# Banded attention and a rational MLP on one core: an issue order planned with slack between the engines

## The chip, the cores and the metric

The kernel runs on one core of a Trainium2 chip. A core has five engines that run their own instruction streams in order: TensorE (PE; its weight loads are shown apart as PEld), VectorE (DVE), ScalarE (ACT), GpSimd (POOL) and SyncE (SP), which here only issues DMAs. They wait for each other on semaphores. The metric is the device time of one execution in microseconds (us), the median of several.

## The reference

Attention over 8 batches, 8 heads, 576 positions and 64 dimensions in float32, causal with a window of 128 and a linear bias by head, and on its result, 4608 tokens of 512 numbers, an MLP with 2048 hidden numbers and a rational function in place of an activation:

```python
scores = scale * np.matmul(q, k.transpose(0, 1, 3, 2))
mask = (rel >= 0) & (rel < window)
scores = np.where(mask, scores + bias[None], -1000000000.0)
attn = softmax(scores)
x = (attn @ v).transpose(0, 2, 1, 3).reshape(B * S, H * D)
h = x @ w_in
P = a[0] + a[1] * h + a[2] * h2 + a[3] * h3
Q = 1.0 + np.abs(b[0]) * np.abs(h) + np.abs(b[1]) * h2
out = (P / (Q + 1e-06)) @ w_out
```

## The kernel before

The tokens are 36 blocks of 128. The MLP takes them in 17 tiles (3 blocks, 15 times 2 blocks, 3 blocks); the attention in units of one pair of heads and one or two blocks, for the most part four units for each MLP tile. While the MLP of tile t runs, the attention of tile t + 1 runs in between and writes x (x_hi and x_lo) for it.

To keep float32 accuracy at a faster matmul, numbers are split into a high part and a remainder, and a product takes three matmuls (high by high, high by low, low by high). The weights come as 64-bit words in memory. For tile 0 they are converted to float32 chunk by chunk (`convert`, L554 to L557, 32 steps k: even ones w_in, odd ones w_out) and used as such. Then `split` (L571, L572) makes the high part on ScalarE and the remainder on VectorE or GpSimd, 32 steps again, while tile 1 already uses the first chunks.

An attention unit is a chain: scores on TensorE (L431), a masked copy and the reduction on VectorE (L445, L451), exponentials on ScalarE (L456), sums on VectorE (L464, L465), the division on GpSimd (L466, buffer pr), the transposes on TensorE (L475, to pt), copies and remainders (L478, L480), two selections on GpSimd (L486 makes p_own, L487 p_all), the product with v on TensorE (L498, to px), and x_hi and x_lo (L514, L516). Its inputs are split as well (L387, L388: kq_lo, v_lo).

An MLP step takes two chunks of 128 hidden numbers (a pair; with three blocks one chunk): up matmuls into h (L597), the rational function as a chain over ScalarE, GpSimd and VectorE (L620 to L636), its split into g_h and g_l (L637 on ScalarE, L638 on VectorE), and down matmuls into the accumulators (L653). After the last chunk ScalarE copies each accumulator to a buffer o (L681) and SP stores it (L682); in the last tile both engines copy halves (L678). There are three buffers for h, three for g_h and g_l each, three shared by pr and o, and two accumulators.

The order of all instructions is not written down but planned when the program is built. `Plan.op` takes an operation with its due number, the engines that may run it with a cost in ns, and what it reads and writes. `Plan.order` plays the engines through: an operation is ready when all that it depends on has ended, plus a latency that goes by the two engines; a free engine takes, of the operations ready at that moment whose buffers are free, the one that is due first. The result is the fixed order in which each engine gets its instructions. Due numbers are in us and come from 25 constants: `a_time` (attention), `m_time` (MLP), `c_time` (conversion) and the numbers added to them at each `plan.op`. Some operations also have an earliest time (`after`). So a due number is a rank, not a time at which something runs.

The latencies between engines (ns), and the due numbers of the split and of the copy of an accumulator:

```python
("p", "a"): 203, ("p", "v"): 230, ("g", "a"): 78, ("g", "v"): 90, ("g", "p"): 150,
T = S0 + DS * k          # split step k; the remainder is due at T + 1; after = 1000 * (T - SL)
E = M + ME               # element operations of the MLP, M = m_time of the pair
D = M + ML + LL * end    # down matmuls; the copy is due at D + OE
```

Of the kernel before, what the change touches and what calls it, by code (L numbers as in the profile page):

```python
# [63 lines left out]
class Slot:  # L64


    def __init__(self, pool, bufs, shape, dtype, name, tag, view=None):
        self.pool, self.bufs, self.shape, self.dtype, self.name, self.tag, self.view = pool, bufs, shape, dtype, name, tag, view
        self.ap, self.turn, self.left, self.free = None, None, [], 0.0
# [6 lines left out]
class Plan:  # L76
# [7 lines left out]

    TICK = 10240 / 3

    def __init__(self):
        self.ops, self.last, self.readers = [], {}, {}

    def op(self, due, engines, emit, reads=(), writes=(), after=0.0, follows=(), rows=1.0, sb=False):  # L90
        o = Op()
# [18 lines left out]
    def order(self):  # L110
# [12 lines left out]
        n = 0  # L123

        def lat(a, b):
            return self.LATENCY.get((a, b), 30)

        def push(o):
            for e in o.engines:
                est = o.after  # L130
                for d in o.deps:
                    est = max(est, d.end + (lat(d.engine, e)))
                ready[e].append([est, o.due, self.index[o], o])
# [21 lines left out]
        def can(o, e, t):  # L155

            need = {}
            for s in o.slots:
                if s.turn is None:
                    need.setdefault(s.tag, []).append(s)  # L160
            for tag, new in need.items():
                if kept.get(tag, (o.due, self.index[o])) < (o.due, self.index[o]):
                    return False
                ring = rings.setdefault(tag, [])
                spare = new[0].bufs - len(ring)
                for old in ring:
                    if old.open == 0:
                        at = max(d.end + lat(d.engine, e) for d in old.left)
                        if at <= t:
                            spare += 1  # L170
                        else:
                            wake(at)
                if spare < len(new):
                    return False
            return True

        def take(s, e, t):
            ring = rings.setdefault(s.tag, [])
            s.turn = True
            if len(ring) == s.bufs:  # L180
                closed = [(max(d.end + lat(d.engine, e) for d in x.left), n) for n, x in enumerate(ring) if x.open == 0]
                ring.pop(min(closed)[1])
            ring.append(s)
# [68 lines left out]
def banded_attention_ratio_mlp(ctx: ExitStack, tc: tile.TileContext, kqv, w_in, w_out, ab, bias, ident, out):  # L252
# [8 lines left out]
    NTILE = len(MLP)  # L261


    A0, DA, T0, L0, L1 = -2.801, 1.382, 22.471, 91.007, 25.039
    AOFF, D2, D3, JL, VL = -0.658, 4.239, 7.383, 7.57, 5.798
    LL = 1.731
    ML, ZA, ME, OE = 23.456, 1.02, 2.318, 6.612
    C0, DC, CO, DO, WL = 2.441, 6.349, 21.451, 5.419, 5.627
    S0, DS, SL, AW, BL = 119.413, 2.051, 4.212, 29.151, 3.617

    plan = Plan()

    def slot(pool, shape, dtype, name, tag=None, view=None):
        return Slot(pool, count[id(pool)], shape, dtype, name, tag or name, view)
# [303 lines left out]
    def mlp(t, cs):  # L578
# [76 lines left out]
        end = t == NTILE - 1  # L655
        D = M + ML + LL * end
        for n, c in enumerate(cs):
# [99 lines left out]
```

## Time and profile before

| | |
|---|---|
| median of 3 runs | 1094.45 us (1093.33 to 1094.52) |
| the profiled execution | 1092.51 us, of which the span from the first to the last instruction is 1090.8 us |
| mean granted clock of TensorE | 0.998 of full speed |
| busy: TensorE matmuls, weight loads | 1059.3 us (97%), 902.8 us (83%) |
| busy: VectorE, ScalarE, GpSimd | 942.7 us (86%), 768.4 us (70%), 590.0 us (54%) |

Busy times are unions of instruction intervals. The ends of matmuls are modelled, and they overlap in the pipeline: a matmul is listed with 0.28 us while the next one starts 0.12 us after it. The idle time of an engine is listed with what ended it; a releaser is inferred from the semaphores.

### The profile page before, as it was taken

The page shows a single profiled execution, that of the slowest core. Times are in us where ns is not written, and L with a number is a line of the kernel's source. Part 1 is how long each engine was busy: PE and PEld are TensorE (multiplying, and loading weights), DVE is VectorE, ACT ScalarE, POOL GpSimd, SP SyncE. Part 2 cuts the span into 40 slices and gives each one's busy share as a digit, 9 for nine tenths or more (in the row PEclk, how much of TensorE's full clock was granted, in tenths as well). Part 3 has the DMA queues.
Part 4 walks back from the last instruction along what each step waited for, and adds up shares of the span by engine and source line. Part 5 has one row for each costly group of instructions (what it writes and reads, how often), then busy time and mean ns, then how long its engine had stood idle before and what let it go on. Part 6 is the DMA issues. An engine that isn't in the chain of part 4 may idle for free.

```text
span 1090.8 us, 19735 instructions
## 1 busy us (share of the span) xinstructions
PE 1059.3 (97%) x6827; PEld 902.8 (83%) x6827; DVE 942.7 (86%) x2192; ACT 768.4 (70%) x1786; POOL 590.0 (54%) x579
## 2 busy tenths in 40 slices
PE   7899889999999999999999999999999999999998
PEld 4555468889888988898888888898888888888997
DVE  5899899989888888888888888888988888899785
ACT  6866779767766776677676666666776766677664
POOL 3755599646554554555545455555464555455442
PEclk9999999999999999999999999999999999999999
DMA  9525310111111111111111111111111111110000
GB/s 309 195 100 169 131 68 20 43 63 43 58 45 59 35 59 45 59 43 61 45 49 51 44 45 42 64 39 59 44 64 40 40 49 64 33 63 33 20 1 30
DMA packets 35477, 68.79 MB, mean 63 GB/s; under 512 B 3376, under 2 KB 19632, under 8 KB 35376
## 3 DMA queue, kind: packets, MB, share of 16 engines
q1 hardware_dynamic: 35376, 67.52, 18.1%
q8 instruction: 54, 0.88, 0.3%
q14 instruction: 47, 0.39, 0.1%
HBM read 58.07 MB, written 9.44 MB: 62 GB/s over the span
## 4 chain that ended last, share of the span: by engine, by line
PE 58%; DVE 15%; ACT 6%; POOL 4%; issue 4%; DMA 1%; DVEq 0%; ACTq 0%; POOLq 0%; SPq 0%
PE acc L653 24%; PE h L597 24%; PE px L498 6%; PE sc L431 3%; PE pt L475 2%; DVE g_p L624 2%; DVE g_p L625 2%; DVE h L630 1%; ACT pr L456 1%; DVE pr L451 1%; POOL p_all L487 1%; DVE h L636 1%; DVE g_l L638 1%; DVE g_q L629 1%; ACT g_u L620 1%
## 5 line engine op out<-in xcount | busy, mean ns | idle before, releaser
L597 PE MATMUL h<-x_hi,wi_hi 128*128 128x256 f32 (+1 forms) x1024 | 304.6, 297 | 7.8 <-DVE g_l L638 5.3
L597 PE MATMUL h<-x_lo,wi_hi 128*128 128x256 f32 (+1 forms) x1024 | 291.1, 284 | 0.0
L597 PE MATMUL h<-x_hi,w_lo 128*128 128x256 f32 (+1 forms) x960 | 273.5, 285 | 0.2 <-POOL w_lo L572 0.2
L621 POOL TENSOR_SCALAR g_q<-g_u,babs 128x512 f32<-128x512 f32 (+1 forms) x152 | 117.5, 773 | 275.9 <-ACT g_u L620 269.6
L597 PEld LDWEIGHTS h<-x_hi,wi_hi 128*128 128x128 f32 x1024 | 192.6, 188 | 35.5 <-DVE g_l L638 7.6
L597 PEld LDWEIGHTS h<-x_lo,wi_hi 128*128 128x128 f32 x1024 | 192.7, 188 | 28.8 <-issue 1.4
L653 PE MATMUL acc<-wo_hi,g_h 128*128 128x512 f32 x528 | 208.2, 394 | 0.2 <-ACT o L681 0.2
L623 POOL TENSOR_TENSOR g_q<-g_q,g_u 128x512 f32<-128x512 f32 (+1 forms) x152 | 192.9, 1269 | 8.3
L653 PE MATMUL acc<-w_lo,g_h 128*128 128x512 f32 x495 | 194.8, 394 | 0.0
L653 PE MATMUL acc<-wo_hi,g_l 128*128 128x512 f32 x528 | 185.3, 393 | 0.0
L597 PEld LDWEIGHTS h<-x_hi,w_lo 128*128 128x128 f32 x960 | 180.6, 188 | 0.4 <-POOL w_lo L572 0.4
L626 ACT ACTIVATE g_u<-g_q,guard 128x512 f32<-128x512 f32 (+1 forms) x152 | 106.3, 699 | 82.9 <-POOL g_q L623 82.6
L629 DVE SCALAR_TENSOR_TENSOR g_q<-g_q,h 128x512 f32<-128x512 f32 (+1 forms) x152 | 99.9, 657 | 72.9 <-ACT h L628 70.5
L456 ACT ACTIVATE pr<-pr,st 128x128 f32<-128x128 f32 x288 | 113.0, 394 | 39.7 <-DVE st L451 39.1
L620 ACT ACTIVATE g_u<-h 128x512 f32<-128x512 f32 (+1 forms) x152 | 87.3, 574 | 73.5 <-PE h L597 72.4
L486 POOL TENSOR_SCALAR_AFFINE_SELECT p_own<-p_all 128x1024 fp32r<-128x1024 f32 (+1 forms) x72 | 81.2, 1128 | 104.9 <-DVE p_all L480 104.1
L466 POOL TENSOR_TENSOR pr<-pr,st 128x512 f32<-128x512 f32 (+1 forms) x76 | 77.7, 1022 | 70.0 <-DVE st L465 51.7
L622 ACT ACTIVATE g_p<-h,na 128x512 f32<-128x512 f32 (+1 forms) x152 | 114.8, 755 | 0.3
L624 DVE TENSOR_TENSOR g_p<-h,g_p 128x512 f32<-128x512 f32 (+1 forms) x152 | 100.1, 658 | 16.0 <-ACT g_p L622 14.8
L630 DVE SCALAR_TENSOR_TENSOR h<-g_p,na,h 128x512 f32<-128x512 f32 (+1 forms) x152 | 109.5, 720 | 0.3
L625 DVE SCALAR_TENSOR_TENSOR g_p<-g_p,na,h 128x512 f32<-128x512 f32 (+1 forms) x152 | 108.1, 711 | 0.7
L628 ACT ACTIVATE h<-g_u 128x512 f32<-128x512 f32 (+1 forms) x152 | 87.3, 574 | 29.3 <-DVE g_p L625 16.9
(91 smaller groups left out, 2255.2 us busy)
## 6 DMA issues: line engine op xcount, KB each, us to landing
kqv_raw<-in_kqv SPq DMA_DIRECT2D x64, 512.0 KB, 3.3
out<-o SPq DMA_DIRECT2D x33, 256.0 KB, 2.1
raw_w<-in_w_in SPq DMA_DIRECT2D x16, 512.0 KB, 4.8
raw_w<-in_w_out SPq DMA_DIRECT2D x16, 512.0 KB, 4.8
bias_t<-in_bias SPq DMA_DIRECT2D x44, 64.0 KB, 1.8
kq<-in_kqv SPq DMA_DIRECT2D x4, 320.0 KB, 5.0
kqv_raw<-in_kqv SPq DMA_DIRECT2D x4, 320.0 KB, 2.8
v<-in_kqv SPq DMA_DIRECT2D x4, 192.0 KB, 5.8
```

The source lines that it names most:

```text
L456: nc.scalar.activation(ap(pr)[:, y, :], ap(pr)[:, y, :], AF.Exp, bias=ap(st)[:, y : y + 1], scale=-1.0, accum_out=ap(st)[:, 4 + y : 5 + y])
L597: nc.tensor.matmul(h(n), w[:, k, :], x[:, k, :], start=(k == 0 and m == 0), stop=(k == NKC - 1 and m == len(seq) - 1))
L620: plan.op(E, {"a": act(W, 1)}, lambda e: nc.scalar.activation(v(g_u), v(h_s), AF.Abs), reads=[(h_s, 0)], writes=[(g_u, 0)])
L621: plan.op(E, {"g": tsc}, lambda e: nc.gpsimd.tensor_scalar(v(g_q), v(g_u), ap(babs)[:, 1:2], ap(babs)[:, 0:1], ALU.mult, ALU.add), reads=[ ...
L622: plan.op(E, {"a": act(W, 1, 2) - 20}, lambda e: nc.scalar.activation(v(g_p), v(h_s), AF.Identity, bias=ap(na)[:, 2:3], scale=ap(na)[:, 3: ...
L623: plan.op(E, {"g": ttc}, lambda e: nc.gpsimd.tensor_tensor(v(g_q), v(g_q), v(g_u), ALU.mult), reads=[(g_q, 0), (g_u, 0)], writes=[(g_q, 0)])
L624: plan.op(E, {"v": dve(W)}, lambda e: nc.vector.tensor_tensor(v(g_p), v(h_s), v(g_p), ALU.mult), reads=[(h_s, 0), (g_p, 0)], writes=[(g_p, ...
L625: plan.op(E, {"v": dve(W, 1)}, lambda e: stt(v(g_p), v(g_p), ap(na)[:, 1:2], v(h_s), ALU.add, ALU.mult), reads=[(h_s, 0), (g_p, 0)], write ...
L626: plan.op(E, {"a": act(W, 0, 1)}, lambda e: nc.scalar.activation(v(g_u), v(g_q), AF.Ln, bias=guard, scale=1.0), reads=[(g_q, 0)], writes=[ ...
L629: plan.op(E, {"v": dve(W)}, lambda e: stt(v(g_q), v(g_q), GUARD, v(h_s), ALU.add, ALU.mult), reads=[(g_q, 0), (h_s, 0)], writes=[(g_q, 0)])
L630: plan.op(E, {"v": dve(W, 1)}, lambda e: stt(v(h_s), v(g_p), ap(na)[:, 0:1], v(h_s), ALU.add, ALU.mult), reads=[(g_p, 0), (h_s, 0)], write ...
L653: nc.tensor.matmul(ap(accs[t][i]), x[:, sl], w, start=(c == 0 and part == 0 and m == 0), stop=(c == NFC - 1 and (part == 1 or t == 0) and ...
```

## The change

The planner adds a slack to the latency whenever a result crosses to another engine, by the engine that receives it: 204 ns for TensorE, 35 for VectorE, 13 for ScalarE, 218 for GpSimd. The latency is also used where a ring of buffers is asked whether one is free. All 25 constants of the due numbers and earliest times are others; they and the slack were chosen by how the fixed order does when delays are random. The operations, their costs in the plan, the buffers and the DMAs are the same. (LATENCY has no entries from or to SP: 30 ns are used, and a slack for the receiving engine is added there too.)

```diff
-    def __init__(self):
-        self.ops, self.last, self.readers = [], {}, {}
+    def __init__(self, slack):
+
+        self.ops, self.last, self.readers, self.slack = [], {}, {}, slack
...
         def lat(a, b):
-            return self.LATENCY.get((a, b), 30)
+            return self.LATENCY.get((a, b), 30) + (self.slack.get(b, 0.0) if a != b else 0.0)
...
-    A0, DA, T0, L0, L1 = -2.801, 1.382, 22.471, 91.007, 25.039
-    AOFF, D2, D3, JL, VL = -0.658, 4.239, 7.383, 7.57, 5.798
-    LL = 1.731
-    ML, ZA, ME, OE = 23.456, 1.02, 2.318, 6.612
-    C0, DC, CO, DO, WL = 2.441, 6.349, 21.451, 5.419, 5.627
-    S0, DS, SL, AW, BL = 119.413, 2.051, 4.212, 29.151, 3.617
-
-    plan = Plan()
+    A0, DA, T0, L0, L1 = -3.5, 1.542, 22.056, 90.639, 24.589
+    AOFF, D2, D3, JL, VL = -0.627, 3.694, 6.675, 9.175, 4.671
+    SP, SV, SA, SG = 0.204, 0.035, 0.013, 0.218
+    LL = -1.886
+    ML, ZA, ME, OE = 23.116, 0.956, 0.92, 12.957
+    C0, DC, CO, DO, WL = 2.237, 6.361, 21.961, 5.327, 5.885
+    S0, DS, SL, AW, BL = 120.646, 2.26, 6.993, 24.311, 4.541
+
+    plan = Plan({"p": 1000 * SP, "v": 1000 * SV, "a": 1000 * SA, "g": 1000 * SG})
```

## Rows read from the trace of the kernel before

**Rows 1.** The page: busy time of each engine over the span.

```profile
PE 1059.3 (97%) x6827; PEld 902.8 (83%) x6827; DVE 942.7 (86%) x2192; ACT 768.4 (70%) x1786; POOL 590.0 (54%) x579
```

**Rows 2.** Windows: busy us and instructions by engine, granted clock, DMA share, GB/s.

```profile
0.00:50.00 50.00, 40.10 (x199) 24.49 (x199) 34.13 (x122) 35.40 (x108) 28.75 (x42) 0.97 0.81 275
50.00:150.00 100.00, 94.19 (x364) 53.97 (x365) 94.88 (x219) 73.08 (x167) 58.55 (x66) 1.00 0.35 114
150.00:200.00 50.00, 46.18 (x322) 40.62 (x321) 47.78 (x94) 40.64 (x86) 47.93 (x39) 1.00 0.14 49
200.00:1027.00 827.00, 819.28 (x5654) 730.83 (x5653) 721.21 (x1673) 584.01 (x1357) 432.92 (x409) 1.00 0.14 48
1027.00:1090.80 63.80, 59.55 (x295) 52.90 (x293) 44.72 (x86) 35.31 (x72) 21.90 (x26) 0.99 0.06 21
```

**Rows 3.** Waits, 200 to 1027 us: total us, times, longest us.

```profile
PEld h L597 <- DVE g_l L638: 6.6, 9, 0.7
PEld px L498 <- POOL p_all L487: 5.3, 10, 0.6
PE h L597 <- DVE g_l L638: 4.8, 9, 0.5
PEld pt L475 <- POOL pr L466: 4.5, 16, 0.5
PEld px L498 <- POOL p_own L486: 4.1, 18, 0.5
```

**Rows 4.** Timeline of TensorE, 335 us: start, us, instruction, idle before it.

```profile
335.37 0.39 PE L597 MATMUL h<-x_hi,wi_hi 128*128 128x256 f32 x1 [0.54 <-DVE g_l L638]
```

**Rows 5.** Timeline of TensorE, 332 us: the tile's last down matmuls.

```profile
332.41 0.62 PE L653 MATMUL acc<-wo_hi,g_l 128*128 128x512 f32 x2
```

**Rows 6.** Timeline of ScalarE, 334 to 341 us: the accumulators' copies.

```profile
335.26 0.57 ACT L681 COPY o<-acc 128x512 f32<-128x512 f32 x1
...
339.88 0.58 ACT L681 COPY o<-acc 128x512 f32<-128x512 f32 x1
```

**Rows 7.** Groups of VectorE, 200 to 1027 us: busy us, mean ns, idle before.

```profile
L638 DVE TENSOR_TENSOR g_l<-h,g_h 128x512 fp32r<-128x512 f32 (+1 forms) x115 | 78.5, 682 | 3.3 <-ACT g_h L637 2.7
...
L388 DVE TENSOR_TENSOR v_lo<-kqv_raw,v_hi 128x384 fp32r<-128x384 f32 (+1 forms) x58 | 44.9, 775 | 0.7 <-ACT v_hi L387 0.6
```

**Rows 8.** Line L571, the splits' casts: ns min/median/max, first and last start.

```profile
L571 ACT CAST wi_hi<-w x16: 600/624/642, 119.8 to 187.1; 128x512 fp32r<-128x512 f32 x16
L571 ACT CAST wo_hi<-w x16: 602/614/637, 121.7 to 190.8; 128x512 fp32r<-128x512 f32 x16
```

**Rows 9.** Timeline of GpSimd, 193 to 199 us: the last remainder.

```profile
195.92 1.62 POOL L572 TENSOR_TENSOR w_lo<-w,wo_hi 128x512 fp32r<-128x512 f32 x1
```

**Rows 10.** Waits of TensorE, 0 to 200 us.

```profile
PE h L597 <- DVE g L633: 5.7, 6, 1.6
...
PE pt L475 <- POOL pr L466: 1.8, 4, 0.9
```

**Rows 11.** The chain that ended last, 1060 to 1091 us: start, us, what.

```profile
1076.07 10.50 PE acc L653 x46
```

**Rows 12.** Timeline of VectorE, 1081 to 1088 us: the last g_l.

```profile
1082.35 0.56 DVE L638 TENSOR_TENSOR g_l<-h,g_h 128x384 fp32r<-128x384 f32 x1 [0.60 <-ACT g_h L637]
```

## The prediction, made before the changed kernel was run

> **What bounds the kernel now.** I read the page first: TensorE is busy for 1059.3 us of the 1090.8, and VectorE for 942.7 [rows 1]. Then I cut the span into stages [rows 2]. From 200 to 1027 us (tiles 1 to 15 of the MLP with the attention of the next tile in between) TensorE is busy for 819.28 of 827 us, VectorE for 721.21: this stage is TensorE's, and what an order can win there is only the time that TensorE waits. From 50 to 200 us it is different: VectorE is busy for 94.88 + 47.78 = 142.66 of 150 us, and in the last third of it GpSimd is busy for 47.93 of 50. There TensorE's waits follow from VectorE and GpSimd; an order could win at most what VectorE idles, 150 - 142.66 = 7.3 us. The last stage is 63.8 us of TensorE work with a short end.
>
> Third, the waits of the long stage [rows 3]. The weight loader waits 6.6 us in 9 places for VectorE's g_l (the release of an h buffer), 5.3 us in 10 for p_all, 4.5 us in 16 for pr, 4.1 us in 18 for p_own: 20.5 us in 53 waits, 0.39 us each, none over 0.7. Not all of that is lost to the matmuls, because a load runs ahead of its matmul; the matmul engine's own idle time is 827 - 819.28 = 7.7 us. So the loss lies between 7.7 and 20.5 us, and I take the middle, 14.1. One such wait is the 0.54 us at 335.37 [rows 4]; the last down matmuls of the tile had ended at 333.03, the two accumulators were copied out only at 335.26 and 339.88 [rows 5, 6], and TensorE had nothing but up matmuls, which ran out of h buffers.
>
> **The change part by part.** No instruction's work is added or removed. Plan.order places the same operations, but thinks that a result from another engine reaches TensorE 204 ns later than before, GpSimd 218, VectorE 35, ScalarE 13; and the 25 numbers that make due times and earliest times are others.
>
> *The slack in the long stage.* I add it along the three chains that end in the waits above. MLP, from h to the release of h: L620 0.013, L621 0.218, L626 0.013, L629 0.035, L637 0.013, L638 0.035, TensorE 0.204: 0.531 us. Scores to transpose: L445 0.035, L456 0.013, L464 0.035, L466 0.218, TensorE 0.204: 0.505. Transpose to values: L478 0.013, L480 0.035, L486 0.218, TensorE 0.204: 0.470. The measured means are 6.6 / 9 = 0.73, 4.5 / 16 = 0.28, and 0.53 and 0.23 for the two value waits. What the slack can cover is therefore 9 x 0.531 = 4.8, 10 x 0.470 = 4.7, 4.5 and 4.1: 18.1 us if TensorE has another matmul ready each time. The slack is a delay in the plan alone; the chip's chains stay as long as they are, and the planner fills TensorE's place with another ready matmul, of which there are mostly some (ups, downs, three h buffers, two attention units). But the 9 longest waits are the places where there were none. Bounds: 0 and 18.1 us won. I take half of the 14.1 that is lost: 7.0 us won, since the sizes of slack and wait match and only the filling is open.
>
> Why the plan of before should be late by a few tenths of a us can be seen on VectorE: v_lo (L388, mostly 384 columns, both inputs in SBUF) takes 775 ns in the mean, more than g_l at mostly 512 columns with one input in PSUM, 682 [rows 7]; the plan asks 469 for the former, or 657 when it sees GpSimd busy. The Trainium skill (SBUF — State Buffer, on the shared port pair) says that a VectorE instruction with two SBUF inputs and a GpSimd instruction that reads SBUF shut each other out for a whole instruction. By that rule, which these means bear out, the delay is a matter of chance meetings that no slack of fixed size can remove; the won time would then be nearer to the lower bound, 0, and that is a case of the first rival below.
>
> *The splits of the weights (S0, DS, SL).* Step k is due at S0 + DS k. For the last remainder (k = 31, L572, due 1 later) that is 119.413 + 63.581 + 1 = 184.0 before and 120.646 + 70.06 + 1 = 191.7 after, 7.7 us later; its earliest start goes from 178.8 to 183.7. What counts is when they run: the first cast starts at 119.8, the last at 190.8 [rows 8], 71.0 / 31 = 2.29 us a step. The new due pace of 2.26 is about this pace, the old one of 2.051 was ahead of it; 183.7 lies 7.1 us ahead of the real start of the last, so the earliest start binds nothing. Queued behind a later split are the remainders on VectorE and GpSimd, and TensorE's up matmuls of the last chunk of tile 1: the last remainder starts at 195.92 and takes 1.62 [rows 9]. Bounds: -7.3 us (all of VectorE's idle time of 50 to 200 us gone) and +7.7 us (the last split later by its whole due shift, uncovered). Attention and the downs of tile 1 cover most of it; I take +1.0, near zero as the pace is.
>
> *The head (A0, DA, T0, L0, C0 to WL).* Shifts of 0.2 to 0.9 us in dues, and two of TensorE's longest sums there, 5.7 us for g and 1.8 us for pr [rows 10], would be covered by the same slack. I cost it at 0, because VectorE at 95% hides it; if that cover were gone, 5.7 + 1.8 = 7.5 us would be open, which is the 7.3 bound again.
>
> *Loads (JL, VL, AW, WL, BL).* From 200 us the DMA engines are busy for 0.14 of the time [rows 2]; loads move by 0.3 to 1.6 us in SP's queue and wait there for buffers. Nothing either way.
>
> *Dues inside a tile (L1, AOFF, ZA, D2, D3, ME).* The last attention unit of a tile is due (2.342 / 4) x 50.08 x 1.02 = 29.9 us after the tile's start before, (2.373 / 4) x 49.18 x 0.956 = 27.9 after, its transposes and values 0.5 and 0.7 earlier still; the MLP's element operations 1.4 earlier. Both groups move the same way by 1 to 3 us, so they stand against each other nearly as before: 0, hidden by the matmuls that VectorE's 721 of 827 us stay behind.
>
> *The tile's end (OE, ML).* The copy of an accumulator is due ML + OE after the last pair: 23.456 + 6.612 = 30.1 before, 23.116 + 12.957 = 36.1 after, 6.0 later. It takes a buffer of the ring that the attention's pr also uses (three), and ScalarE takes the lowest due. The next tile's down matmuls stand behind it. At two attention units in flight a third buffer is always left for one copy, and the other already waits 339.88 - 333.03 = 6.9 us [rows 5, 6]. Lower bound 0. Upper: one more wait of 0.73 us at each of 15 ends, 11 us. I take +0.5.
>
> *The last tile (LL).* Downs are due earlier there by 3.6 us, and 0.34 more by ML. After the last up matmul 46 downs take 10.5 us; the last g_l ends at 1082.35 + 0.56 = 1082.9 [rows 11, 12]. The last chunk has 9 of the 46 (2.1 us), so cover lasts to 1076.07 + 8.4 = 1084.5, 1.6 us more than needed. If the backlog shrinks by 3.96, 3.96 - 1.6 = 2.4 us are lost; if not, 0. I take +0.5.
>
> Sum: -7.0 + 1.0 + 0 + 0.5 + 0.5 = -5.0. The profiled execution took 1092.5 us (span 1090.8), so 1087.5 for the same; the median of the runs lies 1.9 above it, and the forecast is 1094.45 - 5.0 = 1089.4.
>
> **The rivals.** *The waits only move:* the order fills one gap and opens another of the same size, or the delays are chance. The sum without the -7.0 is +2.0: 1096.5, no measurable change (about 0.2%, 2.2 us, is what a measurement can tell). For it speaks that the plan already holds latencies of 150 to 200 ns into TensorE, which still had 53 waits; against, that none of the waits is longer than 0.7 us.
>
> *More is won:* the whole 18.1 us, with the other terms: 1094.4 - 16.1 = 1078. For it: the match of slack and wait; against: 7.7 us is all that the matmul engine itself idles.
>
> *Slower, by the tile's end:* the copies lose to the next attention unit at each end, the second copy comes after more than about 8 us rather than 6.9, and the wait on an h buffer becomes 1.5 us instead of 0.73. That is +11 in place of +0.5, and the sum is +5.5: 1100. For it: the 9 longest waits of the stage stand there already; against: ScalarE is busy for only 584 of 827 us, and the third buffer.
>
> *Slower, by the splits:* +7.7 in place of +1.0: 1096.2, at the edge of what can be told. It decides if the last remainder starts after about 200 us.
>
> **How the numbers follow.** The forecast (own range 1085 to 1092) 0.45; more won 0.13; waits only move 0.20; tile's end 0.12; splits 0.10. Faster by over 0.2%: 0.45 + 0.13 = 0.58. Slower: the tile's end, and a little over half of the splits and a quarter of the moved waits, where the terms other than the slack come out above my values: 0.12 + 0.06 + 0.05 = 0.23. The rest, 0.19, is no change. The range leaves out half of the large gain and the dearer part of the tile's end, some 0.15 together: 1081 to 1099.
>
> **What would show it.** From 200 to 1027 us the four waits of the weight loader should sum to 6 to 14 us rather than 20.5, the pitch of a tile fall by about 0.4 us, the matmul engine idle for 4 us or less. The last remainder should start between 192 and 199 us. Accumulators should be copied within 8 us of a tile's last down, and TensorE should wait for L681 no more than now. The last g_l should land before its downs. The forecast is wrong if the four waits stay near 20 us, if tile 1 ends over 3 us later, or if a new wait on L681 appears at the tile ends.

## The result, and the profile after

The changed kernel takes 1083.47 us (1082.26 to 1085.15), against 1093.89 for the kernel before beside it: 0.9907 of its time, with an interval of 0.9890 to 0.9924. The forecast was 1089.4, in a range of 1081 to 1099: right in the sign, but the gain is 10.4 us instead of 5.0. The profiled execution took 1083.98 us, its span 1082.2.

To see where the time went I cut both spans at two events: the first down matmul of tile 2 and the first of tile 16 (numbers 193 and 1537 of the 1680 matmuls of the line that writes acc). The part between them, the middle, is 14 tiles.

| | head | middle | end | span |
|---|---|---|---|---|
| before | 220.9 | 806.0 | 63.9 | 1090.8 |
| after | 227.7 | 789.3 | 65.2 | 1082.2 |
| difference | +6.8 | -16.7 | +1.3 | -8.6 |

So the change won 16.7 us in the middle, 1.2 us a tile, where the forecast had 7.0, and gave part of it back at both ends. Lines of the changed kernel stand two further down than before (L597 is L599 now, L681 is L683).

The windows of the kernel after, with the columns and stretches of [rows 2]:

```profile
0.00:50.00 50.00, 39.03 (x199) 24.68 (x199) 31.45 (x117) 34.13 (x106) 27.27 (x41) 0.97 0.83 275
50.00:150.00 100.00, 92.66 (x345) 51.39 (x346) 91.28 (x208) 71.22 (x158) 53.34 (x62) 0.98 0.35 109
150.00:200.00 50.00, 45.85 (x301) 38.66 (x300) 49.13 (x100) 41.47 (x96) 49.12 (x40) 1.00 0.14 49
200.00:1027.00 827.00, 824.50 (x5737) 742.12 (x5736) 736.92 (x1692) 596.71 (x1368) 440.98 (x419) 1.00 0.15 49
```

From 200 to 1027 us the matmul engine idles for 2.5 us instead of 7.7, and the same stretch holds 83 matmuls more (5737 against 5654). From 50 to 150 us VectorE is busy for 91.28 us instead of 94.88: the new order packs the head less densely.

Waits of the weight loader in the kernel after, 200 to 1027 us, as in [rows 3]:

```profile
PEld sc L433 <- issue: 3.3, 12, 0.4
PEld px L500 <- POOL p_all L489: 2.7, 9, 0.9
PEld h L599 <- DVE g_l L640: 1.8, 3, 0.9
PEld pt L477 <- POOL pr L468: 1.8, 2, 0.9
PEld pt L477 <- issue: 0.6, 2, 0.4
PEld px L500 <- POOL p_own L488: 0.6, 3, 0.2
```

The four waits that summed to 20.5 us in 53 places are 6.9 us in 17. The 12 waits before sc (3.3 us) are new, but the matmuls that they stand before start no later than usual. At a tile's end the two accumulators are now copied one right after the other; timelines of TensorE and of ScalarE in the kernel after, to be read beside [rows 4 to 6]:

```profile
394.93 0.61 PE L655 MATMUL acc<-wo_hi,g_l 128*128 128x512 f32 x2
395.38 0.28 PE L599 MATMUL h<-x_hi,wi_hi 128*128 128x256 f32 x1
```

```profile
396.44 1.07 ACT L683 COPY o<-acc 128x512 f32<-128x512 f32 x2
```

The last down matmuls end at 395.54, the copies start 0.9 us later and are done at 397.5; before, the second copy started 6.9 us after the downs' end. That is one tile's end each. Of the 14 tile ends of the middle, nine were like this one before: the second copy started 7.2 to 8.0 us after the last down had started, and each of these nine ends has one of the nine waits for g_l. After, it starts at most 2.4 us behind it at every end.

### The profile page after: what moved, and what is told of

Its sections match the earlier page's. It is cut to its first block, busy times and chain, and to the rows that moved or that the text cites. A ratio compares the mean times of both kernels' runs of the same rounds, so it can differ in the third digit from the quotient of the medians.

```text
span 1082.2 us, 19767 instructions
## 1 busy us (share of the span) xinstructions
PE 1053.0 (97%) x6827; PEld 902.0 (83%) x6827; DVE 948.6 (88%) x2190; ACT 774.1 (72%) x1786; POOL 589.3 (54%) x581
## 4 chain that ended last, share of the span: by engine, by line
PE 82%; DVE 7%; POOL 3%; ACT 3%; DMA 2%; issue 2%; SPq 0%; DVEq 0%; ACTq 0%; POOLq 0%
PE h L599 34%; PE acc L655 33%; PE px L500 8%; PE sc L433 5%; PE pt L477 2%; DMA raw_w<-in_w_out 1%; POOL pr L468 1%; DVE h L632 1%; POOL w_lo L574 1%; DVE g_p L626 1%; ACT pr L458 1%; DVE cv L558 1%; DVE g_p L627 1%; DVE v_lo L390 1%; DVE w L559 1%
## 5 line engine op out<-in xcount | busy, mean ns | idle before, releaser
L599 PE MATMUL h<-x_hi,wi_hi 128*128 128x256 f32 (+1 forms) x1024 | 302.5, 295 | 1.2 <-DVE g_l L640 1.2
L599 PE MATMUL h<-x_lo,wi_hi 128*128 128x256 f32 (+1 forms) x1024 | 291.0, 284 | 0.0
L599 PE MATMUL h<-x_hi,w_lo 128*128 128x256 f32 (+1 forms) x960 | 274.0, 285 | 1.5 <-DVE w_lo L574 1.5
L599 PEld LDWEIGHTS h<-x_lo,wi_hi 128*128 128x128 f32 x1024 | 192.5, 188 | 31.9 <-issue 0.7
L599 PEld LDWEIGHTS h<-x_hi,wi_hi 128*128 128x128 f32 x1024 | 192.6, 188 | 28.2 <-DVE g_l L640 1.8
L655 PE MATMUL acc<-wo_hi,g_l 128*128 128x512 f32 x528 | 194.3, 394 | 0.3 <-DVE g_l L640 0.3
L599 PEld LDWEIGHTS h<-x_hi,w_lo 128*128 128x128 f32 x960 | 180.6, 188 | 2.4 <-DVE w_lo L574 1.7
L488 POOL TENSOR_SCALAR_AFFINE_SELECT p_own<-p_all 128x1024 fp32r<-128x1024 f32 (+1 forms) x72 | 78.1, 1085 | 89.3 <-DVE p_all L482 88.7
L640 DVE TENSOR_TENSOR g_l<-h,g_h 128x512 fp32r<-128x512 f32 (+1 forms) x136 | 90.9, 669 | 24.3 <-ACT g_h L639 23.4
L639 ACT CAST g_h<-h 128x512 fp32r<-128x512 f32 (+1 forms) x136 | 77.8, 572 | 40.7 <-DVE h L638 40.3
```

Source lines behind the costliest of these rows:

```text
L599: nc.tensor.matmul(h(n), w[:, k, :], x[:, k, :], start=(k == 0 and m == 0), stop=(k == NKC - 1 and m == len(seq) - 1))
L640: plan.op(E, {"v": dve(W)}, lambda e: nc.vector.tensor_tensor(v(g_l), v(h_s), v(g_h).bitcast(F32), ALU.subtract), reads=[(h_s, 0), (g_h, 0 ...
L655: nc.tensor.matmul(ap(accs[t][i]), x[:, sl], w, start=(c == 0 and part == 0 and m == 0), stop=(c == NFC - 1 and (part == 1 or t == 0) and ...
```

## The experiments

With other numbers the planner puts the same work in another order. "The plan's own head" or "middle" below is where the planner itself, on its clock, starts the matmuls at which I cut; the chip is later, since the planner doesn't have all that the chip does.

My theory (A) was that the slack shortens the middle, by covering the waits; its rival (B) that the new constants do, through the tile ends or the earlier attention.

**Slack or constants.** `late_slack` has the constants of before, and the slack counts only for results that end after 200 us of the plan; `early_slack` has the constants of after, and the slack counts only up to there. In both the head keeps the order of its parent nearly to its end.

```diff
-        def lat(a, b):
-            return self.LATENCY.get((a, b), 30) + (self.slack.get(b, 0.0) if a != b else 0.0)
+        def lat(d, b):
+            return self.LATENCY.get((d.engine, b), 30) + (self.slack.get(b, 0.0) if d.engine != b and d.end >= 200000 else 0.0)
...
```

(`early_slack`: `d.end < 200000`.) `constants_alone` is after with all four slacks 0, `slack_alone` before with the slacks of after.

> The constants of before, and the slack only for results that end after 200 us in the plan. I cut the time at the first down matmul of tile 2 and at that of tile 16: head, middle, end. Before: 220.9, 806.0, 63.9 us; after: 227.7, 789.4, 65.1. Theory A (the slack shortens the middle, and the head became longer by the new order there): head 221, middle 788 to 793, end 64: about 1077 us, faster than both. Theory B (the constants shorten the middle, by the copies at the tile ends or the earlier attention): middle 804 to 808, about 1094 us.

> The constants of after, and the slack only for results that end before 200 us in the plan: the head of after, and a middle planned without slack. Theory A: head 228, middle 800 to 808, about 1098 us. Theory B: head 228, middle 789 to 792, about 1084 us.

> The constants of after with no slack at all. Theory A: middle 800 to 808 us. Theory B: middle 789 to 792. The head: if the new constants make it longer by themselves, 228 or more (the plan's own head is 224.0 us here, against 214.5 with the slack and 208.3 for before, so 237); if it is the slack that does, 221.

> The constants of before with the slack everywhere. Theory A: middle 788 to 793 us. Theory B: middle 804 to 808. The head: the plan's own head is 217.1 us here against 208.3 for before, so about 230 if the chip follows the plan; 221 if the slack costs the head nothing.

| | head | middle | end | time | beside it, before |
|---|---|---|---|---|---|
| late_slack | 225.2 | 789.6 | 65.1 | 1080.44, ratio 0.9868 (0.9853 to 0.9883) | 1094.6 |
| early_slack | 227.5 | 801.3 | 62.3 | 1092.83, ratio 0.9986 (0.9977 to 0.9996) | 1094.6 |
| constants_alone | 245.1 | 799.4 | 62.3 | 1108.52, one execution | 1094.6 |
| slack_alone | 227.7 | 788.7 | 65.1 | 1083.17, one execution | 1094.6 |

Three expectations were missed beside the middle: the heads of `late_slack` (225.2 instead of 221) and of `constants_alone` (245.1 instead of 237), both taken up below, and the time of `early_slack`, 5 us shorter than the 1098 expected. The slack makes the middle: 788.7 and 789.6 us with the constants of before, 789.3 with those of after. The constants without it stop at about 800. Theory A holds; theory B accounts for at most 5 to 7 of the 16.7 us, and the runs below show that orders without slack scatter by that much. In both runs of that kind, `early_slack` and `constants_alone`, all but one of the nine waits for g_l are gone from the middle, but those for p_own have grown from 4.1 us to 7.5 and 5.9. All 25 new constants together are worth nothing beside the slack: `slack_alone` takes as long as the kernel after, as far as one execution can tell. And the late slack with the old constants beats both kernels: its interval lies below that of the kernel after, 0.9890 to 0.9924.

**How much slack, and for whom.** All four on the constants of before, from 200 us of the plan on: the slacks halved, doubled, TensorE's alone, GpSimd's alone. The edit is the line of the constants, for instance for the first:

```diff
-    SP, SV, SA, SG = 0.204, 0.035, 0.013, 0.218
+    SP, SV, SA, SG = 0.102, 0.0175, 0.0065, 0.109
```

> As late_slack (constants of before, slack from 200 us of the plan on), with all four slacks halved: 102, 17.5, 6.5 and 109 ns. The chains then carry 0.24 to 0.27 us. Theory A, by the sizes (the slack covers each wait up to its own sum along the chain): of the 53 waits of 0.39 us some 0.25 each, 12 of 18 us: middle 794 to 798 us. Theory C (any slack, or any other order, removes the waits, and size does not matter): 788 to 791.

> As late_slack with all four slacks doubled (408, 70, 26 and 436 ns). The plan itself grows: its middle from 778.5 to 785.5 us. Theory A: the waits of the loader, already at 7 us, cannot fall by more than that, and the plan's own gaps cost 7 us: middle 790 to 797 us, end 1 to 6 us longer. If chance delays far larger than 0.5 us were still being paid, the middle would fall below 787.

> As late_slack with TensorE's slack of 204 ns alone, the other three 0. Theory A by chains: TensorE's own 0.204 is two fifths of each chain's 0.47 to 0.53 us: 53 x 0.2 = 10.6 us: middle 794 to 798 us. If only the last step into TensorE matters: 788 to 791. If GpSimd's slack does the work: 802 or more.

> As late_slack with GpSimd's slack of 218 ns alone. Theory A by chains: the other two fifths, middle 794 to 798 us. If only the last step into TensorE matters: 802 to 807, as before.

| | middle | the plan's own middle | gain in the middle | time (one execution; beside it, before 1094.77) |
|---|---|---|---|---|
| none (before) | 806.0 | 779.8 | | |
| late_gpsimd | 802.0 | 780.4 | 4.0 | 1089.69 |
| late_half | 798.7 | 779.0 | 7.3 | 1091.88 |
| late_tensor | 797.5 | 778.3 | 8.5 | 1087.42 |
| late_slack | 789.6 | 778.5 | 16.4 | 1080.44 (median of four; beside it, before 1094.6) |
| late_double | 797.1 | 785.5 | 8.9 | 1090.25 |

Half the slack wins a little less than half (7.3 of 16.4; one order repeats within 1.0 us, as shown below), TensorE's part and GpSimd's part sum to 12.5 of the 16.4. Under theory A, TensorE's alone meets its expectation and GpSimd's alone misses it by 4 us (794 to 798); the middle with half the slack lies 0.7 us above its expectation, that with the double 0.1 us. The gain grows with the size up to the size of the waits and is lost again beyond: doubled, the plan itself leaves holes. The plan's own middle hardly differs between the first five; the plan can't see what the chip shows.

**The parts of the prediction that were priced without a row.** `oe_alone` is before with OE = 12.957; `split_old` is after with S0, DS and SL of before; `before_again` is the kernel before once more; `mid_slack` is `late_slack` with the slack only up to 970 us of the plan, `200000 <= d.end < 970000`.

> The kernel before with one constant of after, OE 12.957 in place of 6.612, and no slack. The prediction's rival (copies lose to the attention at the tile ends): middle 815 to 820 us. Theory A: 802 to 808, an accident of order apart. Theory B (the later due puts the two copies together and frees the accumulators): 789 to 797. The head, whose plan is 210.6 us against 208.3: 221 to 226.

> The kernel after with the three constants of the weight splits (S0, DS, SL) of before. If the later splits made the head longer: head 221 to 223 us. If the slack and the other constants did: 226 to 229, as in after (227.7); the plan's own head is 215.0 against 214.5. The middle 788 to 792 under theory A, whatever the splits do.

> The kernel before, unchanged, for the scatter of one profile. Five kernels with the head order of before had heads of 222.6 to 226.6 us where before had 220.9: if that is scatter, 221 to 227 here; if before's head is always short, 220 to 222. The middle should be 804 to 808 us.

> The constants of before, with the slack only for results that end between 200 and 970 us of the plan: head and last tile planned as before, the middle as in late_slack. Middle 788 to 792 us, end 63 to 64.5 instead of 65.1: 1078.5 to 1081 us, 0.985 to 0.988 of before, faster than after; if the end order of late_slack does not matter, the same as late_slack (0.9868).

| | head | middle | end | time | beside it, before |
|---|---|---|---|---|---|
| oe_alone | 225.7 | 807.9 | 64.2 | 1099.58, one execution | 1093.2 |
| split_old | 227.9 | 787.6 | 65.2 | 1082.39, one execution | 1093.2 |
| before_again | 223.1 | 805.0 | 63.9 | 1093.72, one execution | 1093.2 |
| mid_slack | 224.1 | 790.3 | 64.8 | 1078.95, ratio 0.9866 (0.9849 to 0.9882) | 1093.2 |

`oe_alone`: the middle is 1.9 us longer than in before, within theory A's 802 to 808 and far from the rival's 815 to 820 and theory B's 789 to 797. The later due does change the tile ends: the second copy is over 7 us late at six of them instead of nine, and six waits for g_l are left. But the waits for p_all and p_own together grow from 9.4 to 16.0 us: what is won in one place is lost in another. The loader's waits in it, 221 to 1030 us:

```profile
PEld px L500 <- POOL p_all L489: 8.4, 16, 0.8
PEld px L500 <- POOL p_own L488: 7.6, 21, 1.3
PEld h L599 <- DVE g_l L640: 4.4, 6, 0.7
PEld pt L477 <- POOL pr L468: 4.3, 14, 0.6
...
PEld acc L655 <- ACT o L683: 0.2, 1, 0.2
```

`split_old`: the head is as long with the old splits; the later splits are not what lengthened it. Its middle lies 0.4 us below what was expected. `before_again` gives the scatter of one profile: the middle repeats within 1.0 us, the head less well. Eight executions with the head order of before have heads of 220.9 to 226.6 us, 223.7 in the mean; the profile that the prediction rested on had the shortest. After's head order gave 227.7 and 227.5, so it costs about 4 us, not 6.8. The waits of the loader repeat too; `before_again`, 221 to 1026 us:

```profile
PEld h L597 <- DVE g_l L638: 6.5, 9, 0.7
PEld px L498 <- POOL p_all L487: 5.7, 12, 0.6
PEld px L498 <- POOL p_own L486: 4.2, 19, 0.5
PEld pt L475 <- POOL pr L466: 3.7, 14, 0.5
```

These are nearly the numbers of [rows 3] again, kind by kind. The long instructions come back one by one as well: from 220 us on, the same 24 of 58 sums of L464 take over 0.3 us in both profiles of the kernel before, and the same 10 of 57 v_lo of L388 over 0.9. What TensorE waits for is not chance, but a fixed disagreement between plan and chip. `mid_slack` can't be told from `late_slack`; its end of 64.8 us misses the expectation of 64.5 at most.

**What the slack pays for.** If the lateness is the same each time, better prices in the plan should do what the slack does. On back-to-back work the pitch of most operations in the trace of before is within 5% of the plan's cost; of those that were dearer I took the four farthest off, all of them operations of VectorE or GpSimd: L464 (273 ns instead of 80), the two remainders of L388 (770 and 749 instead of 736 and 469), L486 (1258, set as 1261, instead of 1087 at full size). The spread of two of them in the kernel before, 200 to 1027 us (ns, min/median/max):

```profile
L464 DVE TENSOR_TENSOR st<-st,tiny x59: 147/159/871, 208.0 to 1007.5; 128x4 f32<-128x4 f32 x55, 128x2 f32<-128x2 f32 x4
```

```profile
L388 DVE TENSOR_TENSOR v_lo<-kqv_raw,v_hi x58: 409/558/1608, 208.8 to 1002.0; 128x384 fp32r<-128x384 f32 x54, 128x256 fp32r<-128x256 f32 x4
```

`priced_both` sets these prices in the plan from tile 3's attention on, without slack, with the constants of before; for L388 the plan's factor of 1.4 beside a busy GpSimd is left out with them. `priced_vector` and `priced_gpsimd` set a part.

```diff
...
-        plan.op(A + 1, {"v": 80}, lambda e: nc.vector.tensor_tensor(
+        plan.op(A + 1, {"v": 80 if t < 3 else 273}, lambda e: nc.vector.tensor_tensor(
...
-            plan.op(A + D2 + 0.5, cost, lambda e: nc.gpsimd.affine_select(
+            own_cost = cost if t < 3 else {"g": cost["g"] + 0.17 * parts * n * P}
+            plan.op(A + D2 + 0.5, own_cost, lambda e: nc.gpsimd.affine_select(
```

> The kernel before, no slack, its constants; only the plan's costs of four operations are set to the pitch that the trace of before shows in the middle stage, for the attention units of tile 3 and later: L464 273 ns instead of 80, the remainders L388 770 and 749 instead of 736 and 469 (or 1.4 times that when the plan sees GpSimd busy), L486 1261 instead of 1087. Theory D (the chip is late against the plan in the same places each time, and these mispriced collisions of VectorE and GpSimd are why; the slack only pays for them in a lump): middle 789 to 796 us. Theory E (the lateness is spread over many steps or is chance, and only a margin helps): middle 801 to 808.

> As priced_both, with the costs of VectorE's operations alone (L464, L388). Theory D: these are two of the three collisions on the chain from scores to transposes; middle 794 to 801 us. Theory E: 801 to 808.

> As priced_both, with GpSimd's L486 alone. Theory D: the waits on p_own and p_all (9.4 of the 20.5 us) shrink, the others stay; middle 797 to 803 us. Theory E: 801 to 808.

| | middle | time | beside it, before |
|---|---|---|---|
| priced_both | 799.2 | 1089.98, ratio 0.9958 (0.9947 to 0.9970) | 1093.86 |
| priced_vector | 806.1 | 1097.3, one execution | 1093.86 |
| priced_gpsimd | 804.5 | 1096.0, one execution | 1093.86 |

The mean prices win 6.8 us together and next to nothing singly. Theory D fails in size: 799.2 is between the two expectations, and no better than `constants_alone` with its 799.4. In the rows above most instructions take about the median and some up to 0.7 us (L464) or 1.05 us (v_lo) more; a mean price fits neither, and the waits are in other places now. The loader of `priced_both`, 221 to 1026 us:

```profile
PEld pt L477 <- POOL pr L468: 9.4, 21, 1.1
PEld px L501 <- POOL p_own L489: 2.5, 5, 1.4
```

Over all runs the middle is 799.2 to 807.9 us in the seven orders without slack there and 787.6 to 790.3 in the five with the whole of it. Which operation's lateness each of the 53 waits came from is not settled.

## Why the prediction was right and where it was wrong

*What bounds the kernel.* Right. The middle is TensorE's; the gain came out of its waits there, and VectorE and GpSimd got busier in it (736.92 instead of 721.21 us of 827), not less.

*The slack in the long stage, -7.0.* The mechanism was right and its size wrong: -16.7 measured. The term was half of a loss of 14.1 us, and the half is what failed. What a wait costs can be read from the starts of the matmuls. The wait of [rows 4], in the timeline of TensorE before:

```profile
334.56 0.28 PE L597 MATMUL h<-x_hi,w_lo 128*128 128x256 f32 x1
335.37 0.39 PE L597 MATMUL h<-x_hi,wi_hi 128*128 128x256 f32 x1 [0.54 <-DVE g_l L638]
```

From start to start 0.81 us passed where 0.12 is the pitch: 0.69 lost, 0.54 listed, because a matmul is listed with 0.28 us at that pitch. The Trainium skill (Perfetto Trace Analysis, Tensor Engine Instruction (MATMUL, LD_WEIGHTS)) says that the profiler estimates when a matmul ends and doesn't observe it, which agrees with these rows. (TensorE had not only up matmuls there, as the prediction has it: scores ran from 333.31 us.)

I took the same difference, from start to start less the usual distance of two such matmuls, at every wait of the four kinds in the middle. It sums to 12.6 us in 52 waits before and 2.1 us in 14 after. So the loss of 14.1 was about right, by luck, for neither end was a bound: the listed idle time of the matmul engine at these waits, 7.1 us, hides 5.5 more, and the 18 waits of the loader for p_own sum to 4.1 us and cost the matmuls 0.4. Half of it was wrong: 10.5 of the 12.6 us came back. TensorE had another matmul ready nearly always, also at the tile ends, where the prediction took it that there was none (nine waits for g_l before, one after). The other 6 us had no term in the prediction. About 4 of them were delays of at most 0.11 us each before transposes and products with v (4.7 us in the middle before, 0.9 after), too short for the list of waits; the rest is not traced. That 16.7 comes near the bound of 18.1, which the chains' sums gave for the listed waits alone, is therefore luck too.

*Chance meetings as the reason for a gain near 0.* Wrong: with the Trainium skill's rule of the shared port (SBUF — State Buffer, Who interferes with whom) I took the meetings of VectorE and GpSimd for chance. The long tails of L464 and L388 agree with the rule. But the order is fixed, so the long instructions come in the same places each time, as `before_again` shows, and a slack of fixed size could cover most of the waits. That the waits come from these meetings is not shown.

*The splits, +1.0, and the head, 0.* The splits cost nothing (`split_old` 227.9 against 227.7). The last remainder starts at 201.8 us, later than the 192 to 199 forecast, with the old splits at 202.2: the whole head is late. The head's own term was the wrong one: costed at 0, it is +4.0 in the means and +6.8 between the two profiles. So tile 1 ended over 3 us later, one of the prediction's signs of being wrong. What failed is the argument that VectorE's 95% hides an order's effect there. The order can also make VectorE wait: from 50 to 150 us it is busy for 92.1 to 96.0 us in the eight executions with the head order of before, for 91.3 and 91.6 in the two with that of after. The slack alone lengthens the head by 4.0 us, the constants alone by 21 (one execution each), both together by 4.0. The plan knew: the first down of tile 2 is at 208.3 us in the plan of before, at 217.1, 224.0 and 214.5 in these three.

*The tile's end, +0.5, and its rival.* The rival's +11 did not come: the middle of `oe_alone` is 1.9 and 2.9 us longer than in the two profiles of before, and after copies sooner, not later. A cost of the copies in after is not seen. *The last tile, +0.5.* +1.3 by this cut. No wait for g_l appeared: 39 downs follow the last up matmul rather than 46, and the last g_l is in time. The chain that ended last, and VectorE's timeline, after:

```profile
1069.06 8.94 PE acc L655 x39
```

```profile
1075.24 0.56 DVE L640 TENSOR_TENSOR g_l<-h,g_h 128x384 fp32r<-128x384 f32 x1 [0.60 <-ACT g_h L639]
```

The two runs with the new LL and no slack at the end have 62.3 us; the others, `late_double` with its 67.9 apart, 63.4 to 65.2 with and without slack there. What the slack costs the end and what LL wins is not settled by this cut.

*The rivals.* That the waits only move is refuted for the kernel after by the sums, though `oe_alone` is a case of it; both slower mechanisms by `oe_alone` and `split_old`. *More is won* was the nearest in its middle term, by the luck told above.

With measured terms the sum is -16.7 + 4.0 + 1.3 = -11.4 us, against -10.4 of the medians.

## What to carry to other kernels

In a stage that one engine bounds, an order planned with exact latencies makes that engine wait a few tenths of a us wherever the chip is late, and the plan doesn't show it. A margin along the chains that end at the bounding engine, in sum about as large as these waits, removed most of them here at no cost to the plan's own middle; on the last step into TensorE alone it won half. In the head, where several engines are full, the same margin cost 4 us, so give it by stage. Take what a wait costs from the starts of the matmuls around it: the listed idle time of the matmul engine says too little, the waits of the weight loader say too much.

## What was not expected of the hardware

In `constants_alone` the head of 245.1 us is not the order's doing alone. Its windows, with the columns of [rows 2]:

```profile
150.00:155.00 5.00, 2.48 (x18) 1.95 (x20) 3.53 (x19) 3.85 (x15) 1.04 (x1) 0.72 0.05 15
155.00:165.00 10.00, 6.96 (x34) 5.17 (x32) 7.46 (x21) 7.79 (x22) 6.43 (x6) 0.63 0.07 26
165.00:176.00 11.00, 7.95 (x51) 6.40 (x51) 7.29 (x11) 5.78 (x11) 10.07 (x7) 1.00 0.28 97
176.00:183.00 7.00, 5.56 (x30) 5.12 (x31) 6.74 (x10) 4.71 (x8) 7.00 (x7) 0.51 0.00 1
```

Its TensorE had waited there in single pieces (among them 2.02 us before 150.83, 1.63 before 174.06, 2.76 before 177.44), and the granted clock fell to the lower of its two levels, 1.2 of 2.4 GHz, for parts of this stretch and nearly all of 176 to 183 us. The Trainium skill (TensorE: Matmul & The Clock Gate, What's actually happening) says that the clock is set by how busy the engine has been; the rows agree. A long wait can thus be paid twice: the four transposes at 177.44 us took 1.12 us, where four of the kernel after, at 397.19 us and a granted clock of 1.00, took 0.60. In the middle the granted clock was 1.00 in before and after, with waits under 1 us; `late_double` had waits of 2.46 us before 967.58 and 3.59 before 1020.65, and a granted clock of 0.83 from 965 to 975 us and 0.66 from 1020 to 1025.
